# A prologue re-chained per output, w1 cut 3 x 128 + 64, and w2 in seven row halves: two parallel blocks on one Trainium2 core

## The chip, the cores and the metric

The kernel runs on one core of a Trainium2 chip (trn2). The metric is the device time of one execution in microseconds; before the change the median of three runs is 178.09 us. Engines are named as in the profile: PE is TensorE (PEld its weight loads), DVE is VectorE, ACT is ScalarE, POOL is GpSimd, SP is SyncE; SPq and ACTq are the two queues that start DMAs here.

## The reference

Token count S = 2048, width D = 448, 16 heads of 28, MLP width 1792, all in bf16. `_A_ref` is a linear attention with a softmax feature map, `_B_ref` a shifted mixing block with an MLP; both read the same normalised input.

```python
xn = _layernorm(x)
return x + _A_ref(xn, A_wqkv, A_w_phi, A_wo) + _B_ref(xn, B_w1, B_w2, B_w3, B_w4)

# A: q, k, v from xn @ wqkv, per head:
pq, pk = q @ w_phi, k @ w_phi
phi_q = concat(softmax(pq), softmax(-pq)); phi_k = concat(softmax(pk), softmax(-pk))
kv = phi_k^T @ v; z = sum_s phi_k
o = (phi_q @ kv) / (phi_q @ z + 1e-6); A = o @ wo

# B: (c = 112; g0..g3 are the four feature quarters, each shifted by its own number of tokens)
h = gelu(layernorm(xn) @ w1)
g0 = h[:, 0:c] one token later;  g1 = h[:, c:2c] one token earlier
g2 = h[:, 2c:3c] two later;      g3 = h[:, 3c:] two earlier
x1 = xn + concat(g0, g1, g2, g3) @ w2
B = x1 + gelu(layernorm(x1) @ w3) @ w4
```

The kernel normalises xn once and uses it for both, since a second normalisation of a normalised row is nearly the identity.

## The kernel before

The 2048 tokens are 16 tiles of 128; four tiles are a group of 512. Every operation goes through a `Recorder`: the Python order of the calls is each engine's order. `solve` works out the waits from what each operation reads and writes. For SBUF it keeps 32-byte pieces of a row, apart for the upper and lower 64 partitions but no finer than that; for PSUM it keeps whole banks. `mm` is line 203, `tr` (a transpose on PE) line 207, `act` 211, `ew` (DVE and POOL) 215, `dma_t` (a DMA transpose) 218, `dma` 221.

PE works in two row halves of 64: two matmuls with different halves run side by side. `lap_pair` splits the 448 rows of a contraction into chunks of 128 at rows 0, 128, 192 and 320 (the second and third overlap), so that an output costs seven half matmuls, four in one half and three in the other. A pair of outputs is played as two steps: the lower rows of the first beside the upper rows of the second, then the rest. A bank written from one row half has to be done before the other half adds to it; `solve` makes that a wait of PE on itself.

The prologue normalises x (`ln1_stats`, `ln1_apply`): per tile DVE takes the statistics (BATCH_NORM_STATS2, BATCH_NORM_AGGREGATE into `mv`), POOL adds epsilon and raises to the power -1/2 (`ln_scale`, into `rs`), and DVE applies both (TENSOR_SCALAR into `xn`). In the kernel before, the statistics of tile i+1 stand on DVE before the apply of tile i (but for tile 3):

```python
for i in range(10):
    ln1_stats(i, 1, 0)
    if i not in (0, 4):
        ln1_apply(dve, i - 1)
```

Tiles 0 to 11 are transposed on PE (`xn_T`) and copied to `xnT` by ACT; tiles 12 to 15 by four DMA transposes on SPq (`xn_Td`). Out of `xnT` come v (`v_pair`, `v_out`: 12 of 16 tiles here), w1 (`w1_pair`, `w1_out`: four chunks of 112 features by four groups of tokens, gelu on ACT, into `hT`), and the folded weights w_q·w_phi and w_k·w_phi (`fold_pair`, FO). `spin` is dummy matmuls at the start. SPq holds, in this order: loads of x and wv, eight DMA transposes of wqkv (`load_wT`), the four `xn_Td`, then `load_rest`: w2, w3, wo, w4.

Then come eight passes (`ps`), each with a pair of k tiles, a quarter of a q group, and one side job: a pair of w2 tiles (`w2_pair`, four chunks of 112 features in halves of 64 and 48 rows, the token shift being only another column of `hT`) or of the last v tiles. The rest interleaves w3 pairs, the attention numerators and the final sums, and ends with the stores.

The lines that the prediction's steps touch are `ln1_stats`, `ln1_apply` and `ln_scale` (DVE and POOL, line 215), `xn_Td` and `load_rest` (SPq, 218 and 221), `w1_out` (ACT, 211), and the first w1 matmul of group 3, which needs tiles 12 to 15.

Of the kernel before, what the change touches and what calls it, by code (L numbers as in the profile page):

```python
# [9 lines left out]
F32 = mybir.dt.float32  # L10
# [213 lines left out]
def bass_parallel_sum__linear_kernel_hedgehog__mixer_s_mlp__prompt_kernel(  # L224
# [5 lines left out]
    assert (S, D, H, DH, F) == (2048, 448, 16, 28, 1792)  # L230
    NT, NG, KC, NC, NM, FC, HP = 16, 4, 4, 4, 4, 14, 32
    CR = 112
    SHIFTS = [1, -1, 2, -2]
    HW = S + 16
    x2d, out2d = A_x[0], out[0]

    es = ExitStack()
    with es:
# [3 lines left out]
        def region(name, nbytes):  # L242
            nbytes = -(-nbytes // 64) * 64
            total[0] += nbytes
            h = es.enter_context(nc.sbuf_tensor(name, [128, nbytes // 2], BF16))
            R.track(h, nbytes)
            return h

        def view(h, cols, dt=BF16, at=0):
            a = h[:, at // 2:at // 2 + cols * DTB[dt] // 2]  # L250
            return a if dt == BF16 else a.bitcast(dt)
# [13 lines left out]
        xn = new("xn", NT * 512).rearrange("p (t d) -> p t d", t=NT)  # L265
        xnT_r = region("xnT", KC * S * 2)
        xnT = view(xnT_r, KC * S).rearrange("p (c s) -> p c s", c=KC)
        hT_r = region("hT", NM * HW * 2)
        hT = view(hT_r, NM * HW).rearrange("p (m s) -> p m s", m=NM)
        phik_r = region("phik", NT * 1024 * 2)  # L270
        phik = view(phik_r, NT * 1024).rearrange("p (t g e) -> p t g e", t=NT, e=HP)
        vaug_r = region("vaug", NT * 512 * 2)
        vaug = view(vaug_r, NT * 512).rearrange("p (t c) -> p t c", t=NT)
        gT = new("gT", 2 * KC * 512).rearrange("p (b c s) -> p b c s", b=2, c=KC)
        eq_lo = new("eq_lo", NC * 2 * 1024).rearrange("p (c s f) -> p c s f", c=NC, s=2)
# [7 lines left out]
        w1 = view(w1_r, KC * D).rearrange("p (c d) -> p c d", c=KC)  # L283
        w2 = new("w2", NM * D).rearrange("p (m d) -> p m d", m=NM)
        wo = new("wo", KC * D).rearrange("p (c d) -> p c d", c=KC)
        w3 = new("w3", KC * F).rearrange("p (c f) -> p c f", c=KC)
# [13 lines left out]
        rs = new("rs", NT * 8, F32).rearrange("p (t c) -> p t c", t=NT)  # L300
        st2 = new("st2", NT * 8, F32).rearrange("p (t c) -> p t c", t=NT)
        mv2 = new("mv2", NT * 8, F32).rearrange("p (t c) -> p t c", t=NT)
# [47 lines left out]
        def load_lap(dst, src, engs=("SP", "SP")):  # L350
            for h in range(2):
                R.dma(dst[:, 2 * h:2 * h + 2, :], src[192 * h:192 * h + 256, :].rearrange("(c p) d -> p c d", p=128), engs[h])

        load_x(0, 1)
        load_x(1, 1, "ACT")
        load_x(2, 1)
        load_lap(wv, A_wqkv[:, 896:1344], ("ACT", "SP"))
        load_x(3, 1, "ACT")
        load_x(4, 2)
        load_x(6, 2)  # L360

        def load_wT(t):
# [6 lines left out]

        def load_rest():  # L370
            R.dma(w2[0:CR, :, :], B_w2.rearrange("(m p) d -> p m d", p=CR))
            load_lap(w3, B_w3)
            load_lap(wo, A_wo)
            R.dma(w4[:, :, :], B_w4.rearrange("(c p) d -> p c d", p=128))

        vp = vaug.rearrange("p t (h e) -> p (t h) e", e=HP)

        R.op("ACT", lambda e: e.preload_act_table_set("gelu_apprx_tanh_and_others"), [], [])
        load_lap(w1, B_w1, ("ACT", "ACT"))
        load_x(8, 4, "ACT")  # L380
        load_x(12, 4, "ACT")
        R.dma(wphi[0:CR, :, :], A_w_phi.rearrange("(c q) e f -> (q e) c f", q=4), "ACT")
        R.ew(pool, "memset", ident[:, :], 0.0)
# [4 lines left out]
        R.ew(pool, "memset", hT[:, :, 0:2], 0.0)  # L388
        R.ew(pool, "memset", hT[:, :, S + 2:S + 4], 0.0)
        busy = gT[:, 0, 0, 0:256]  # L390
# [130 lines left out]

        def v_out(i, b, eng="ACT"):
            vd = vaug[:, i:i + 2, :].rearrange("p t (h e) -> p t h e", e=HP)[:, :, :, 0:DH]
            vs = two(2 * b)[:, :, 0:D].rearrange("p t (h e) -> p t h e", e=DH)
            if eng == "ACT":
                R.act(vd, vs, ACT.Copy)
            else:
                R.ew(dve, "tensor_copy", vd, vs)

        def w1_pair(g, m, b):  # L530
            return lap_pair([banks[2 * b + k][0:CR, :] for k in range(2)],
                         lambda k, kc, lo, hi: w1[lo:hi, kc, CR * (m + k):CR * (m + k) + CR],
                         lambda k, kc, lo, hi: xnT[lo:hi, kc, 512 * g:512 * g + 512])

        def w1_out(g, m, b):
            R.act(hT[0:CR, m:m + 2, 2 + 512 * g:2 + 512 * g + 512], two(2 * b)[0:CR, :, :], ACT.Gelu_apprx_tanh)

        def w2_pair(i, b):
            def side(k, lo, hi):
                r = []  # L540
                for m in range(NM):
                    c0 = 2 + 128 * (i + k) - SHIFTS[m]
                    r.append((banks[2 * b + k][:, 0:D], hT[lo:hi, m, c0:c0 + 128], w2[lo:hi, m, :]))
                return r
            return (lambda: row_pairs(side(0, 0, 64), side(1, 64, CR), True),
                    lambda: row_pairs(side(1, 0, 64), side(0, 64, CR)))

# [172 lines left out]

        for i in range(10):
            ln1_stats(i, 1, 0)
            if i not in (0, 4):
                ln1_apply(dve, i - 1)
            if i == 3:
                ln1_apply(dve, 3)
        phi_blocks()

        ln1_stats(10, 2, 0)
        ln1_apply(dve, 9)  # L730
        ln1_stats(12, 2, 0)
        ln1_apply(dve, 10)
        ln1_apply(dve, 11)
        ln1_stats(14, 1, 0)
        ln1_apply(dve, 12)
        ln1_apply(dve, 13)
        ln1_stats(15, 1, 0)
        ln1_apply(dve, 14)
        ln1_apply(dve, 15)
        for i in range(12, NT):  # L740
            xn_Td(i)
        load_rest()
        late_3()

        vps = {i: v_pair(i, b) for i, b in ((0, 2), (2, 3), (4, 3), (6, 2), (8, 2), (10, 3))}
        wps = {(g, m): w1_pair(g, m, b) for g, m, b in ((0, 0, 0), (0, 2, 1), (1, 0, 0), (1, 2, 1), (2, 0, 0),
                                                        (2, 2, 1), (3, 0, 0), (3, 2, 2))}
        fps = {(t, m): fold_pair(t, m, b) for t, m, b in ((1, 0, 2), (1, 2, 3), (0, 0, 1), (0, 2, 3))}

        def V(i, k):  # L750
            return (vps[i][k],)

        def W(g, m, k):
            return (wps[g, m][k],)

        def FO(t, m, k):
            return (fps[t, m][k],)

        spin(19, 256)
        play([(xn_T, 0, 0), (spin, 3, 256), (xn_T, 1, 1), (spin, 4, 256), V(0, 0), (xn_T, 2, 0), V(0, 1), (xn_T, 3, 1),  # L760
              (spin, 2, 256), V(2, 0), (v_out, 0, 2), W(0, 0, 0), (xn_T, 4, 2), V(2, 1), (v_out, 2, 3),
              W(0, 2, 0), (xn_T, 5, 2), W(0, 0, 1), (xn_T, 6, 3), W(0, 2, 1), (xn_T, 7, 2), (w1_out, 0, 0, 0),
              (w1_out, 0, 2, 1), V(4, 0), V(6, 0), V(4, 1), (v_out, 4, 3), V(6, 1), (v_out, 6, 2),
              W(1, 0, 0), (xn_T, 8, 3, 2), W(1, 2, 0), W(1, 0, 1), (xn_T, 10, 3, 2), W(1, 2, 1),
              (w1_out, 1, 0, 0), (w1_out, 1, 2, 1), V(8, 0), V(10, 0), V(8, 1), (v_out, 8, 2), V(10, 1),
              (v_out, 10, 3), W(2, 0, 0), W(2, 2, 0), FO(1, 0, 0), W(2, 0, 1), (w1_out, 2, 0, 0), FO(1, 0, 1),
              FO(1, 2, 0), W(2, 2, 1), (w1_out, 2, 2, 1), FO(1, 2, 1), W(3, 0, 0), FO(0, 0, 0), W(3, 2, 0),
              FO(0, 0, 1), FO(0, 2, 0), W(3, 2, 1), (w1_out, 3, 2, 2), W(3, 0, 1), (w1_out, 3, 0, 0), FO(0, 2, 1)])

# [10 lines left out]
        for ps in range(8):  # L780
            k, q = k_pair(2 * ps, 1), q_pair(ps // 2, 2 * (ps % 2), 0)
            kind, i = side[ps]
            w = {"w": w2_pair, "v": v_pair}[kind](i, 2)
            k[0]()
            if ps > 2:
                kv_tile(2 * ps - 6)
                kv_tile(2 * ps - 5)
            w[0]()
            k[1]()
            for s in range(2):  # L790
                k_exp(2 * ps, 1, s)
            q[0]()
            w[1]()
            if kind == "w":
                w2_out(i, 2)
            if kind == "v":
                v_out(i, 2, "DVE" if i == 12 else "ACT")
            q[1]()
            for s in range(2):
                q_exp(2 * ps, 0, s)  # L800
            k_norm(2 * ps)
            if kind == "w" and i < 8:
                w2_norm(i)
            for t in g_at.get(ps, ()):
                g_apply(t)
                g_T(t)
# [91 lines left out]
```

## Time and profile before

| | us |
|---|---|
| runs | 178.50, 178.09, 177.61 (median 178.09) |
| span of the profiled execution, first to last instruction | 175.9 |
| median of the runs less that span | 2.2 |
| PE busy | 170.8 (97%) |
| DVE / ACT / POOL busy | 110.0 / 82.5 / 93.7 |

The execution that was profiled has a span of 175.9 us. Its whole time is that span and the start and end that lie around it, which the profile doesn't show; the median run is 2.2 us over the span, and that is taken for what lies around. The busy time of PE counts dummy matmuls too. Times in the trace are microseconds from the start of the span. In the rows, a shape 64\*128 is 64 rows by 128 columns of weights; xN is a number of instructions, and what stands in square brackets is the idle time of the engine before the first of them and who ended it.

### The profile page before, as it was taken

The page shows a single profiled execution, that of the slowest core. Times are in us where ns is not written, and L with a number is a line of the kernel's source. Part 1 is how long each engine was busy: PE and PEld are TensorE (multiplying, and loading weights), DVE is VectorE, ACT ScalarE, POOL GpSimd, SP SyncE. Part 2 cuts the span into 40 slices and gives each one's busy share as a digit, 9 for nine tenths or more (in the row PEclk, how much of TensorE's full clock was granted, in tenths as well). Part 3 has the DMA queues.
Part 4 walks back from the last instruction along what each step waited for, and adds up shares of the span by engine and source line. Part 5 has one row for each costly group of instructions (what it writes and reads, how often), then busy time and mean ns, then how long its engine had stood idle before and what let it go on. Part 6 is the DMA issues. An engine that isn't in the chain of part 4 may idle for free.

```text
span 175.9 us, 5042 instructions
## 1 busy us (share of the span) xinstructions
PE 170.8 (97%) x2198; PEld 94.7 (54%) x2198; DVE 110.0 (63%) x252; ACT 82.5 (47%) x92; POOL 93.7 (53%) x130
## 2 busy tenths in 40 slices
PE   7899999998999999999999999999999999999993
PEld 4466557744565555665554554554545545545551
DVE  4799906699899697615776981644427415474621
ACT  2368874997779877926324422223214222224000
POOL 3666670016799999860358489460620723523740
PEclk9999999999999999999999999999999999999999
DMA  5994158990001120121011372134611310311331
GB/s 172 330 240 79 35 97 255 390 345 15 0 4 30 34 60 4 30 55 39 4 34 40 79 74 59 48 82 89 93 30 57 82 34 0 86 30 30 86 100 34
DMA packets 32981, 14.87 MB, mean 85 GB/s; under 512 B 24704, under 2 KB 32448, under 8 KB 32960
## 3 DMA queue, kind: packets, MB, share of 16 engines
q1 hardware_dynamic: 30192, 12.64, 29.6%
q10 hardware_dynamic: 2768, 1.92, 3.4%
q8 instruction: 17, 0.28, 0.7%
q14 instruction: 4, 0.03, 0.1%
HBM read 7.08 MB, written 1.84 MB: 51 GB/s over the span
## 4 chain that ended last, share of the span: by engine, by line
PE 91%; DVE 6%; issue 1%; POOL 0%; ACT 0%; DVEq 0%
PE bank L203 90%; DVE vaug L215 1%; DVE st L215 1%; DVE ksum L215 1%; PE bank L207 1%; DVE xn L215 1%; DVE mv L215 0%; ACT xnT L211 0%; POOL rs L215 0%; DVE rks L215 0%; DVEq L176 0%; DVE gT L215 0%; POOL mv L215 0%
## 5 line engine op out<-in xcount | busy, mean ns | idle before, releaser
L211 ACT ACTIVATE phik<-bank 128x1024 bf16<-128x1024 f32 (+1 forms) x44 | 42.3, 984 | 62.4 <-PE bank L203 62.4
L203 PE MATMUL bank<-gT,w 64*128 64x512 bf16 x392 | 50.1, 377 | 0.0
L215 DVE TENSOR_TENSOR vaug<-bank,vaug 128x464 f32<-128x464 f32 (+3 forms) x65 | 32.6, 512 | 23.0 <-PE bank L203 21.4
L203 PE MATMUL bank<-w,phik 64*128 64x448 bf16 (+1 forms) x420 | 45.0, 349 | 0.0
L215 POOL TENSOR_TENSOR xnT<-vaug 128x196 bf16<-128x196 f32 (+1 forms) x32 | 18.1, 585 | 46.8 <-DVE vaug L215 46.8
L203 PEld LDWEIGHTS bank<-w,phik 64*128 64x128 bf16 (+1 forms) x420 | 21.7, 94 | 21.2 <-issue 0.4
L215 POOL TENSOR_TENSOR phik<-phik,rks 128x1792 bf16<-128x1792 bf16 x8 | 25.7, 3212 | 10.8 <-DVE rks L215 10.8
L203 PEld LDWEIGHTS bank<-gT,w 64*128 64x128 bf16 x392 | 18.6, 94 | 17.0 <-ACT hi L211 0.3
L215 POOL TENSOR_TENSOR vaug<-xn,xtok 128x448 f32<-128x448 bf16 x16 | 16.2, 1031 | 0.2 <-DVE vaug L215 0.2
L215 DVE TENSOR_REDUCE ksum<-phik 128x64 f32<-128x1792 bf16 x8 | 16.0, 2006 | 0.0
L203 PE MATMUL bank<-w,hT 64*128 64x448 bf16 (+1 forms) x128 | 15.0, 349 | 0.5 <-DVE vaug L215 0.5
L215 DVE RECIPROCAL vaug<-bank 128x16 f32<-128x16 f32 x16 | 4.1, 257 | 18.0 <-PE bank L203 18.0
L203 PE MATMUL bank<-xnT,wpq 64*128 64x512 bf16 x112 | 14.9, 376 | 0.0
L203 PE MATMUL bank<-xnT,w 64*112 64x512 bf16 x112 | 14.8, 380 | 0.0
L203 PE MATMUL bank<-wpk,xnT 64*128 64x448 bf16 x112 | 13.4, 349 | 0.0
L203 PE MATMUL bank<-wo,xnT 64*128 64x448 bf16 (+1 forms) x106 | 13.4, 349 | 0.0
L215 DVE TENSOR_TENSOR xn<-bank,xn 128x512 bf16<-128x512 f32 (+1 forms) x16 | 9.2, 616 | 6.3 <-PE bank L203 6.3
L203 PE MATMUL bank<-wv,xnT 64*128 64x448 bf16 x112 | 13.0, 350 | 0.1
L215 POOL TENSOR_TENSOR rs<-mv,mhalf 128x1 f32<-128x1 f32 (+2 forms) x18 | 12.2, 679 | 1.5
L215 POOL TENSOR_SCALAR g_tok<-xn,rs 128x512 bf16<-128x512 bf16 x16 | 12.1, 767 | 0.2
L211 ACT ACTIVATE xnT<-bank 128x512 bf16<-128x512 bf16 x12 | 7.0, 603 | 6.3 <-PE bank L207 6.3
L215 DVE BATCH_NORM_STATS2 st<-xtok 128x6 f32<-128x448 bf16 x16 | 9.8, 615 | 0.0
(62 smaller groups left out, 168.0 us busy)
## 6 DMA issues: line engine op xcount, KB each, us to landing
w<-in_B_w_dram SPq DMA_DIRECT2D x2, 896.0 KB, 7.1
out_dram<-vaug SPq DMA_DIRECT2D x15, 112.0 KB, 1.9
w<-in_B_w_dram SPq DMA_DIRECT2D x1, 1568.0 KB, 12.0
xtok<-in_A_x_dram ACTq DMA_DIRECT2D x2, 448.0 KB, 7.3
xtok<-in_A_x_dram SPq DMA_DIRECT2D x2, 224.0 KB, 5.7
w<-in_B_w_dram ACTq DMA_DIRECT2D x2, 224.0 KB, 5.8
wo<-in_A_wo_dram SPq DMA_DIRECT2D x2, 224.0 KB, 8.4
w<-in_B_w_dram SPq DMA_DIRECT2D x1, 392.0 KB, 3.8
```

The lines of the kernel that those rows point to most:

```text
L203: self.op("PE", lambda e: e.matmul(out, lhsT, rhs, start=start, stop=stop, skip_group_check=True), [out], [lhsT, rhs], tile=self._tile(lhsT))
L207: self.op("PE", lambda e: e.transpose(out, in_, ident), [out], [in_, ident], tile=self._tile(in_))
L211: self.op("ACT", lambda e: e.activation(out, in_, func, **kw), [out], [in_] + aps)
L215: self.op(eng, lambda e: getattr(e, name)(out, *args, **kw), [out], aps)
```

## The change

It changes four things.

1. w1 is computed for features 0 to 383 in three chunks of 128 (`z_h` for tiles 0 to 3 one tile at a time, `z_w1` for groups 1 to 3), and for features 384 to 447 with tokens as rows (`z_rest`): 64 columns for each tile, read at tokens two further on, gelu into `hR`, and one DMA transpose for eight tiles (`rest_T`) into `hRT`.
2. A chunk of 128 features now crosses the borders of the shift quarters at 112, 224 and 336. So rows 64 to 127 of each chunk are copied within SBUF, shifted, by six DMAs on SPq for each half of the tokens (`h_shift`). w2 takes seven row halves for each tile in place of eight.
3. The prologue is played as one chain (`zip_in`): the lower rows of each output beside the upper rows of the output before. The normalisation's instructions are put into that chain (`L`), and five of the v copies go to DVE.
4. Loads change places: w1 and x(3) to other slots, `load_w2` behind `rest_T(0)`, w3 and w4 later, wo late into the buffer of wv.

```diff
-        load_lap(wv, A_wqkv[:, 896:1344], ("ACT", "SP"))
-        load_x(3, 1, "ACT")
-        load_x(4, 2)
+        load_half(wv, wv_d, 0, "ACT")
+        load_half(wv, wv_d, 1)
+        load_half(w1, B_w1, 0, "ACT")
+        load_x(3, 1)
+        R.op("ACT", lambda e: e.preload_act_table_set("gelu_apprx_tanh_and_others"), [], [])
+        load_half(w1, B_w1, 1)
+        load_x(4, 2, "ACT")
         load_x(6, 2)
+        load_x(8, 4, "ACT")
+        load_x(12, 4)
+        R.dma(wphi[0:CR, :, :], ...)
...
+        def zip_in(make):
+            prev, n4 = tail[0] if tail[0] else (None, True)
+            lo = make(LO, KCS[0] if n4 else (0, 1, 3)) if make else []
+            hi = prev(HI, KCS[0] if n4 else KCS[1]) if prev else []
+            for k in range(max(len(lo), len(hi))):
+                for step in (lo[k:k + 1], hi[k:k + 1]):
+                    for mms in step:
+                        for out, l, r, first in mms:
+                            R.mm(out, l, r, first, False)
+            tail[0] = (make, not n4) if make else None
...
+        def z_rest(h, b):
+            def make(rows, kcs):
+                lo, hi = rows
+                return [[(banks[b][:, 64 * j:64 * j + 64],
+                          xnT[lo:hi, kc, 1024 * h + 128 * j + 2:1024 * h + 128 * j + 130], w1[lo:hi, kc, REST:D],
+                          rows == LO and n == 0 and j == 0) for j in range(8)] for n, kc in enumerate(kcs)]
+            return make
...
+        def rest_T(h):
+            R.dma_t(hRT[:, 4 * h:4 * h + 4, :], hR[:, 512 * h:512 * h + 512])
+
+        def h_shift(gg):
+            for m, r0, r1, q in ((0, 64, 112, 0), (0, 112, 128, 1), (1, 64, 96, 1), (1, 96, 128, 2), (2, 64, 80, 2),
+                                 (2, 80, 128, 3)):
+                s0 = max(0, 1024 * gg + SHIFTS[q])
+                s1 = min(S, 1024 * gg + 1024 + SHIFTS[q])
+                c0 = OFF + s0 - SHIFTS[q]
+                R.dma(hT[r0:r1, m, s0:s1], hT[r0:r1, m, c0:c0 + s1 - s0])
 
         def w2_pair(i, b):
-            def side(k, lo, hi):
+            def side(k, hi, rest):
                 r = []
-                for m in range(NM):
-                    c0 = 2 + 128 * (i + k) - SHIFTS[m]
-                    r.append((banks[2 * b + k][:, 0:D], hT[lo:hi, m, c0:c0 + 128], w2[lo:hi, m, :]))
+                for m in range(NH):
+                    if hi:
+                        h = hT[64:128, m, 128 * (i + k):128 * (i + k) + 128]
+                    else:
+                        c0 = OFF + 128 * (i + k) - SHIFTS[m]
+                        h = hT[0:64, m, c0:c0 + 128]
+                    lo = 64 * hi
+                    r.append((banks[2 * b + k][:, 0:D], h, w2[lo:lo + 64, m, :]))
+                if rest:
+                    r.append((banks[2 * b + k][:, 0:D], hRT[lo:lo + 64, i // 2, :], w2[lo:lo + 64, NH, :]))
                 return r
...
-        for i in range(10):
-            ln1_stats(i, 1, 0)
-            if i not in (0, 4):
-                ln1_apply(dve, i - 1)
...
-        for i in range(12, NT):
-            xn_Td(i)
-        load_rest()
...
         spin(19, 256)
...
+        play([L(("s", 0), ("s", 1), ("a", 0), ("s", 2), ("a", 1), ("s", 3), ("a", 2), ("a", 3)),
+              (xn_T, 0, 0), (spin, 3, 256), (xn_T, 1, 1), ZV(0), ZV(1), (xn_T, 2, 0), ZH(0), EV(0),
+              L(("s", 4), ("a", 4)), (xn_T, 3, 0), ZV(2), EV(1, "DVE"), ZH(1),
+              L(("s", 5), ("a", 5)), (xn_T, 4, 0), ZV(3), ZH(2), EV(2),
+              L(("s", 6), ("a", 6)), (xn_T, 5, 0), ZV(4), EV(3), ZH(3), EV(4, "DVE"),
+              L(("s", 7), ("a", 7)), (xn_T, 6, 0), ZV(5), (w1_out, 0, 0, 2), (w1_out, 0, 2, 4, 1),
+              L(("s", 8), ("s", 9), ("a", 8), ("a", 9)), ZV(6), EV(5), (xn_T, 7, 0), ZV(7), EV(6, "DVE"), (phi_blocks,),
+              L(("s", 10, 2), ("a", 10), ("a", 11)), (xn_T, 8, 0, 2),
+              ZW(1, 0), EV(7), ZW(1, 1), ZW(1, 2), Z(z_rest(0, 7)), (w1_out, 1, 0, 2),
+              L(("s", 12, 2), ("a", 12), ("a", 13)), (xn_T, 10, 0, 2), ZV(8), (w1_out, 1, 2, 4, 1), (rest_out, 0, 7), (h_shift, 0),
+              ZV(9), EV(8, "DVE"),
+              L(("s", 14, 2), ("a", 14), ("a", 15)), *[(xn_Td, i) for i in range(12, NT)], (rest_T, 0), (load_w2,),
+              (late_3,), ZV(10), EV(9), ZV(11), EV(10, "DVE"), ZW(2, 0), EV(11), ZW(2, 1), FO(1, 0, 0), FO(1, 0, 1), ZW(2, 2), (w1_out, 2, 0, 2),
+              FO(1, 2, 0), FO(1, 2, 1), ZW(3, 0), (w1_out, 2, 2, 4, 1), (load_lap, w3, B_w3), FO(0, 0, 0), ZW(3, 1), FO(0, 0, 1),
+              ZW(3, 2), (w1_out, 3, 0, 2), FO(0, 2, 0), Z(z_rest(1, 5)), (w1_out, 3, 2, 4, 1), (h_shift, 1), FO(0, 2, 1), Z(None), (rest_out, 1, 5),
+              (rest_T, 1), (load_w4,)])
...
+            if ps == 5:
+                load_lap(wo, A_wo)
```

`ZV(i)` is v of tile i, `ZH(t)` the three chunks of w1 of tile t, `ZW(g, m)` a chunk of w1 of group g, `EV` the copy of a v tile out of PSUM. `load_half` and `load_lap` issue the same DMAs by halves.

## The prediction

> **What bounds the kernel now.** I read the page first, then the trace in order of time: the prologue on VectorE and GpSimd, the queue of SP, the waits of TensorE, and stretches of the last microseconds for the clock.
>
> ```profile
> PE 170.8 (97%) x2198; PEld 94.7 (54%) x2198; DVE 110.0 (63%) x252; ACT 82.5 (47%) x92; POOL 93.7 (53%) x130
> PE 91%; DVE 6%; issue 1%; POOL 0%; ACT 0%; DVEq 0%
> ```
>
> TensorE is busy for 97% of the span and carries 91% of the chain that ended last, so columns taken from it count, provided that its operands still come in time. Who delivers them in the prologue is in the timeline of VectorE (first fence) and GpSimd (second):
>
> ```profile
> 8.67 0.62 DVE L215 BATCH_NORM_STATS2 st<-xtok 128x6 f32<-128x448 bf16 x1
> 9.32 0.18 DVE L215 BATCH_NORM_AGGREGATE mv<-st 128x2 f32<-128x6 f32 x1
> 9.42 0.60 DVE L215 BATCH_NORM_STATS2 st<-xtok 128x6 f32<-128x448 bf16 x1
> 10.05 0.18 DVE L215 BATCH_NORM_AGGREGATE mv<-st 128x2 f32<-128x6 f32 x1
> 10.45 0.41 DVE L215 TENSOR_SCALAR xn<-xtok,mv,rs 128x512 bf16<-128x512 bf16 x1 [0.22 <-POOL rs L215]
> ...
> 22.64 0.41 DVE L215 TENSOR_SCALAR xn<-xtok,mv,rs 128x512 bf16<-128x512 bf16 x1 [0.72 <-POOL rs L215]
> ```
>
> ```profile
> 9.59 0.19 POOL L215 TENSOR_SCALAR mv<-mv 128x1 f32<-128x1 f32 x1 [1.29 <-DVE mv L215]
> 9.87 0.55 POOL L215 TENSOR_TENSOR rs<-mv,mhalf 128x1 f32<-128x1 f32 x1
> ```
>
> Tile 4 begins at 8.67 and is applied by 10.86: 2.19 us, of which 0.95 (9.50 to 10.45) is the trip to GpSimd. In that gap VectorE does the statistics of tile 5. So tiles follow each other every 1.1 us, and tile 15 is done at 23.05. The timeline of SP shows what comes behind it:
>
> ```profile
> 6.29 10.96 SPq L218 DMA_TRANSPOSE hi<-in_A_wqkv_dram  x8
> 20.57 5.48 SPq L218 DMA_TRANSPOSE xnT<-xn  x4
> 26.09 1.63 SPq L221 DMA_DIRECT2D w<-in_B_w_dram  x3
> ```
>
> The four transposes of tiles 12 to 15 take 1.3 us each on the queue; the last is issued at 24.8 and lands at 27.3, by the DMA rows 2.7 us from issue to landing:
>
> ```profile
> out_dram<-vaug SPq DMA_DIRECT2D x15, 112.0 KB, 1.9
> w<-in_B_w_dram SPq DMA_DIRECT2D x1, 392.0 KB, 3.8
> xnT<-xn SPq DMA_TRANSPOSE x4, 2.7
> ```
>
> TensorE starts w1 of group 3, which needs them, at 27.70 with next to no wait:
>
> ```profile
> 27.70 1.07 PE L203 MATMUL bank<-xnT,w 64*112 64x512 bf16 x8
> ```
>
> So the cover of this chain is only some 0.4 us thick.
>
> **The change, part by part.**
>
> *TensorE's columns.* 28 matmuls of 448 columns take 2.85 us (15.01); without the last one's 0.35 that is 0.093 each, and by columns 0.106 for 512. w1 loses 28 of 112 half matmuls of 512 columns: 2.97. The token rows add 112 of 64 columns. Sixteen transposes of 64 columns take 0.40, the last one 0.19, so 0.014 each: 1.57. w1 gains 1.4 us. w2 goes from 128 to 112 halves: 16 x 0.093 = 1.5 us. The per-tile form of w1 has the same columns and four times the weight loads, which lie beside matmuls. Extra waits of TensorE on itself, about 27 hand-overs in the chain, are 0.03 to 0.2 us each (0.2 is one step of a row half, two times 0.093): V(0)'s second half began 0.06 after the first one's last matmul had ended (8.12 + 0.35 to 8.53). All of this lies ahead of w1 of group 3. What ends there is decided below, and TensorE waits anyway, so gain and loss there are both worth nothing; with that cover gone, it would be 1.4 less about 1.
>
> *VectorE's order.* The built order of the changed kernel has, from tile 4 on, statistics and apply of the same tile next to each other, with a wait on GpSimd between; nothing else stands in the gap. Five copies of v (from the 128x896 cast of 1.06 and the 128x224 of 0.38: 0.61 each) join the same queue. x(3) moves from third on ACT's queue (landed at 6.14) to fourth on SP's; by the landings beside it at 6.9, so tile 3 is done at 9.1 instead of 8.75. Then, in order: tile 4, 2.2, 11.3; copy, 11.9; tiles 5 and 6, 16.3; copy, 16.9; tile 7, 19.1. Tiles 8 and 9 overlap by one step: two statistics (1.6), the second trip (about 1.0), one apply (0.4): 3.05, 22.15. Copy and mask product (0.38), 23.15. Tiles 10 and 11 have their statistics together and one trip for both: 15.52 to 18.22 for the same work in the trace, then 0.7 for two applies, so 3.45: 26.6. Tiles 12 and 13: 30.05. Copy: 30.65. Tiles 14 and 15: 34.1. That is 11 us later than 23.05.
>
> *SP's queue.* Six shifted copies now stand before the four transposes. The first waits for the gelu of group 1. That needs: tile 9 at 22.15, transposes 0.4, then three chunks of w1 less the last half, 2.4, gelu 1.03, some 0.2 for semaphores: 26.2. Each second copy waits for the landing of the one before, since both touch the same rows' half. A copy inside SBUF is not in the trace: the nearest row is the 112 KB store with 1.9 us; ends are 1.5 (the 56 KB store) and 2.6 (112 KB load). I take 1.9, for its 96 KB or less with no queue before it: landings at 28.1, 30.5, 32.9, the last issue done at 33.4. Then transposes at 33.4, 34.7, 36.0 and 37.3; tile 15 (34.1) is not in their way any more. The last lands 2.7 later: 40.0. **Group 3's w1 starts at 40.0 in place of 27.7: +12.3** (with 1.5: 38.7; with 2.6: 42.1; without any copies: tile 15 at 34.1, two transposes, 37.8).
>
> *Loads.* `rest_T(0)` is issued at 38.6, w2 at 39.9. By the 3.8 us row it lands at 43.7, and the first w2 matmul is due at 45: just hidden. w3 and w4 (7 and 12 us) are needed 20 us later and more; wo, into the place of wv, not before the final sums. The second six copies (from about 44 to 52) serve w2 tiles from 7 on.
>
> *From there on.* Behind group 3's start lay 3.7 us until the first k matmul (31.41). Now there are half the second token rows, single-sided ends and waits on itself: about 4.3, +0.6. In the passes w2 saves 1.5, but at 41.03 TensorE already waited 0.48 for VectorE, which feeds the banks there; so I take 1.2.
>
> *The clock.* TensorE will stand idle from about 36 to 40. Of such a stand the trace has only its end: the last matmul starts at 173.16, and
>
> ```profile
> core 0: us, PE busy (x) PEld busy (x) DVE busy (x) ACT busy (x) POOL busy (x), PEclk, DMA share, GB/s
> 1.20:4.90 3.70, 3.65 (x18) 2.53 (x19) 2.26 (x6) 1.28 (x1) 1.80 (x9) 1.00 0.85 249
> 175.00:176.00 1.00, 0.00 (x0) 0.00 (x0) 0.00 (x0) 0.00 (x0) 0.00 (x0) 0.84 0.04 10
> ```
>
> a mean clock of 0.84 in the last stretch is half speed for its last 0.3 us, so the clock fell some 2.5 us after the last matmul. At the start 18 dummy matmuls took 3.70 us, 0.21 each, against 0.11 for those at 5.9. A fall would thus cost up to half of 3.7, 1.9 us; none costs 0. Four microseconds are longer than 2.5, but that one row says nothing of a stand with work on both sides. I take half, 0.9. The Trainium skill ("TensorE: Matmul & The Clock Gate", Part 1) says that the clock halves after an idle window of about 3.4 us that runs freely, and warns of gaps as long between bursts. By that rule a stand of 4 us holds a whole window about once in six, an estimate from that page, and the sum would mostly be 189.8. By the row alone the fall would be sure, and the sum 191.7.
>
> Sum: 175.9 + 12.3 + 0.6 - 1.2 + 0.9 = 188.5 of span. The span of before stands 2.2 under the median of the runs; I keep that: **190.7 us**.
>
> **The rivals.**
>
> *The normalisation ends last, not the copies on SP.* If copies land in 1 us or less, the transposes of 14 and 15 wait for tile 15 and land at 37.8: 2.2 less, 188.5, or 187.6 with no fall of the clock. For it: the copies are small. Against: every DMA in the trace needs 1.5 or more. Chance 0.13.
>
> *w2 lands late.* w3's 1.8 MB go out right behind w2 and share its engines. If w2 needs 7.1 as the w3 loads did, the first w2 matmul waits until 47: +2, 192.7. It decides from 5.1 us on. Against: w2 was first in the same row of loads before, and landed in 3.8. Chance 0.08.
>
> *Faster: the trip to GpSimd stays hidden.* If the prologue were bound by TensorE alone, w1 and w2 would give 2.9 and the single chain would lose about 1: 176.2. It decides at about 1.4 us per tile from tile 4 on, so that tile 15 were applied by 24. Only a shorter trip could do that, and nothing in the change shortens it: 2.2 for a tile alone is also what tile 0 shows (3.22 to 5.45). Chance 0.03. That the change doesn't do what it says would be this case's opposite: token rows at 0.03 in place of 0.014 each, which eats w1's gain and, under the wait, costs nothing.
>
> **How the numbers follow.** The forecast has 0.76, the rivals 0.13, 0.08 and 0.03. The range goes from 187.0 (normalisation last, no fall of the clock, half a microsecond of error) to 193.5 (copies at 2.6, or w2 late). A measurement of this kernel can tell about 0.5% from no change. All cases but one are slower by 4% or more: faster 0.03, same 0.01, slower 0.96.
>
> **What would show it.** Right: applies of single tiles 2.2 us apart or more, each with some 0.9 idle released by POOL `rs`; tile 15 at about 34; three gaps on SPq released by DMAs of `hT`; the first w1 matmul of group 3 at about 40 after an idle TensorE of some 4 us; TensorE's busy time in the passes 1.5 shorter. Wrong: tile 15 applied before 30, a w1 start before 37, or a second idle stretch before the first w2 matmul.

## The result, and the profile after

The changed kernel takes 194.13 us (median of four runs, 191.76 to 194.4) beside 178.18 for the kernel before: a ratio of 1.086 (95% interval 1.080 to 1.093), 16 us more. The forecast was 190.7, in a range up to 193.5: the direction and the place were right, the size was 3.4 us short. The profiled execution took 194.26 us and has a span of 192.5. Three of the four runs took 194.0 to 194.4 at a mean granted clock of 0.973, the fourth 191.76 at 0.982, which is about one stretch of 3.41 us less at half speed.

From the page of the changed kernel: busy times, the granted clock of TensorE in 40 slices of 4.8 us, and the chain that ended last.

```profile
PE 175.0 (91%) x2323; PEld 92.9 (48%) x2323; DVE 113.3 (59%) x257; ACT 80.8 (42%) x95; POOL 92.3 (48%) x131
...
PEclk9999979966999999999999999999999999999999
...
PE 78%; DVE 8%; DMA 4%; POOL 3%; SPq 2%; ACT 2%; issue 1%; DVEq 0%
```

TensorE's share of the chain falls from 91% to 78%; DMAs, SP's queue, VectorE and GpSimd now stand in it. The clock was lowered in two places, about 23 to 27 us and 40 to 47 us. The busy time of TensorE rises by 4.2 us although it has fewer columns to do: a matmul at half speed counts as busy for twice as long (in the run with all three edits below, whose clock never fell, the same matmuls are busy for 170.0).

The timeline of VectorE, start and length in us:

```profile
7.91 0.63 DVE L215 BATCH_NORM_STATS2 st<-xtok 128x6 f32<-128x448 bf16 x1 [1.34 <-DMA xtok<-in_A_x_dram]
...
9.77 0.41 DVE L215 TENSOR_SCALAR xn<-xtok,mv,rs 128x512 bf16<-128x512 bf16 x1 [0.72 <-POOL rs L215]
...
11.89 0.41 DVE L215 TENSOR_SCALAR xn<-xtok,mv,rs 128x512 bf16<-128x512 bf16 x1 [0.95 <-POOL rs L215]
...
14.53 0.41 DVE L215 TENSOR_SCALAR xn<-xtok,mv,rs 128x512 bf16<-128x512 bf16 x1 [0.95 <-POOL rs L215]
...
16.65 0.41 DVE L215 TENSOR_SCALAR xn<-xtok,mv,rs 128x512 bf16<-128x512 bf16 x1 [0.95 <-POOL rs L215]
...
33.33 0.74 DVE L215 TENSOR_SCALAR xn<-xtok,mv,rs 128x512 bf16<-128x512 bf16 x2 [1.10 <-POOL rs L215]
```

The first row is the late x(3). In the next ones the trip to GpSimd, hidden behind the next tile's statistics before, stands open as 0.95 us of idle in each tile; a tile alone takes 2.1 us and one with a copy behind it 2.6. Tile 15 is done at 34.06, where the forecast had 34.1.

The timeline of SP, then what TensorE waited for longest (total, times, longest), then its first matmul of group 3's w1:

```profile
28.34 8.07 SPq L221 DMA_DIRECT2D hT<-hT  x6
36.46 5.24 SPq L218 DMA_TRANSPOSE xnT<-xn  x4
41.74 1.26 SPq L218 DMA_TRANSPOSE hRT<-gT  x1
43.05 2.95 SPq L221 DMA_DIRECT2D w<-in_B_w_dram  x5
```

```profile
PE bank L203 <- DMA xnT<-xn: 7.6, 1, 7.6
```

```profile
43.15 1.46 PE L203 MATMUL bank<-xnT,w 64*128 64x512 bf16 x6 [7.56 <-DMA xnT<-xn]
```

All four transposes stand behind six shifted copies, though the first two of their tiles had been normalised since 30.2. Group 3's w1 starts at 43.15, 15.45 us later than before; the first k matmul follows at 49.45, 18.04 later.

Stretches of the changed kernel, cut where the clock record changes, each 3.41 us long. The columns wanted are PE busy with its matmuls, and PEclk (third from the right):

```profile
core 0: us, PE busy (x) PEld busy (x) DVE busy (x) ACT busy (x) POOL busy (x), PEclk, DMA share, GB/s
...
16.41:19.83 3.42, 2.36 (x42) 1.18 (x39) 2.20 (x6) 2.38 (x4) 0.94 (x3) 1.00 0.51 95
19.83:23.24 3.41, 1.71 (x34) 0.83 (x36) 2.62 (x8) 0.89 (x3) 1.49 (x4) 1.00 0.02 5
23.24:26.65 3.41, 3.41 (x19) 1.51 (x15) 2.23 (x8) 1.51 (x3) 0.90 (x2) 0.50 0.00 0
33.49:36.90 3.41, 1.98 (x42) 1.22 (x36) 3.20 (x5) 1.05 (x2) 2.33 (x3) 1.00 0.13 31
36.90:40.31 3.41, 0.00 (x0) 0.00 (x0) 0.00 (x0) 0.00 (x0) 0.00 (x0) 1.00 0.54 108
40.31:43.73 3.42, 0.58 (x4) 0.33 (x6) 0.00 (x0) 0.00 (x0) 0.00 (x0) 0.50 0.57 115
43.73:47.14 3.41, 3.41 (x34) 1.74 (x30) 0.24 (x1) 0.60 (x1) 0.00 (x0) 0.50 0.73 159
```

A window that was half busy (1.71 of 3.41) is followed by one at half speed, a window busy for 1.98 is not, and an empty one is. The first fall hits w1 of group 1, on which the shifted copies wait; the second hits w1 of group 3.

### The profile page after: what moved, and what is told of

It reads as the page before. It is cut to its first block, busy times and chain, and to the rows that moved or that the text cites. A ratio compares the mean times of both kernels' runs of the same rounds, so it can differ in the third digit from the quotient of the medians.

```text
span 192.5 us, 5319 instructions
## 1 busy us (share of the span) xinstructions
PE 175.0 (91%) x2323; PEld 92.9 (48%) x2323; DVE 113.3 (59%) x257; ACT 80.8 (42%) x95; POOL 92.3 (48%) x131
## 4 chain that ended last, share of the span: by engine, by line
PE 78%; DVE 8%; DMA 4%; POOL 3%; SPq 2%; ACT 2%; issue 1%; DVEq 0%
PE bank L203 78%; DMA xtok<-in_A_x_dram 3%; DVE st L215 2%; POOL rs L215 2%; DVE xn L215 2%; SPq L218 2%; DMA xnT<-xn 1%; DVE vaug L215 1%; DVE ksum L215 1%; DVE mv L215 1%; ACT hT L211 1%; POOL mv L215 1%; SPq L221 1%; DVE wpk L215 1%; ACT xnT L211 1%
## 5 line engine op out<-in xcount | busy, mean ns | idle before, releaser
L215 DVE TENSOR_TENSOR vaug<-bank,vaug 128x464 f32<-128x464 f32 (+3 forms) x65 | 32.6, 512 | 23.0 <-PE bank L203 21.3
L203 PE MATMUL bank<-wv,xnT 64*128 64x448 bf16 (+1 forms) x218 | 32.4, 353 | 1.4 <-ACT xnT L211 0.7
L203 PE MATMUL bank<-xnT,w 64*128 64x128 bf16 (+1 forms) x147 | 19.6, 334 | 7.8 <-DMA xnT<-xn 7.6
L203 PEld LDWEIGHTS bank<-gT,w 64*128 64x128 bf16 x392 | 17.7, 94 | 17.8 <-ACT phik L211 0.4
L203 PEld LDWEIGHTS bank<-wv,xnT 64*128 64x128 bf16 (+1 forms) x218 | 12.1, 94 | 11.5 <-ACT xnT L211 1.6
L203 PEld LDWEIGHTS bank<-xnT,w 64*128 64x128 bf16 x147 | 9.5, 102 | 12.0 <-issue 8.9
L215 POOL TENSOR_SCALAR mv<-mv 128x1 f32<-128x1 f32 (+2 forms) x17 | 3.5, 203 | 20.1 <-DVE mv L215 19.8
L211 ACT ACTIVATE hT<-bank 128x1024 bf16<-128x1024 f32 (+1 forms) x8 | 6.4, 811 | 15.0 <-PE bank L203 14.8
L203 PE MATMUL bank<-w,hT 64*128 64x448 bf16 x96 | 12.1, 349 | 0.5 <-DVE vaug L215 0.5
L215 POOL TENSOR_TENSOR rs<-mv,mhalf 128x1 f32<-128x1 f32 (+2 forms) x17 | 11.7, 689 | 1.4
```

What stands on the lines that cost most here:

```text
L203: self.op("PE", lambda e: e.matmul(out, lhsT, rhs, start=start, stop=stop, skip_group_check=True), [out], [lhsT, rhs], tile=self._tile(lhsT))
L211: self.op("ACT", lambda e: e.activation(out, in_, func, **kw), [out], [in_] + aps)
L215: self.op(eng, lambda e: getattr(e, name)(out, *args, **kw), [out], aps)
```

## The experiments

Two theories of where the 16 us come from. The forecast's: VectorE's order and the copies on SP's queue, one behind the other, delay group 3, and a lowered clock adds to it. The rival: the single chain itself (single-sided ends, waits of TensorE on itself) costs a good part. The table has the marks of each profiled execution in us: end of tile 15's apply, first shifted copy, first of the four transposes, first w1 of group 3, first k matmul; then the time of the run or median.

| kernel | tile 15 | copies | transposes | group 3 | first k | time |
|---|---|---|---|---|---|---|
| before | 23.05 | none | 20.57 | 27.70 | 31.41 | 178.18 |
| changed | 34.06 | 28.34 | 36.46 | 43.15 | 49.45 | 194.13 |
| statistics ahead | 29.06 | 26.26 | 34.73 | 41.48 | 47.70 | 192.5 |
| copies behind | 33.91 | 39.45 | 29.77 | 38.53 | 45.74 | 194.63 |
| finer pieces | 33.14 | 25.88 | 30.42 | 38.02 | 44.99 | 189.79 |
| half-row dummies | 32.93 | 25.68 | 33.78 | 41.92 | 49.05 | 194.1 |
| full-row dummies | 33.22 | 25.95 | 34.02 | 40.82 | 45.20 | 190.0 |
| all three | 26.54 | 31.46 | 24.51 | 31.59 | 35.97 | 181.42 |
| all three, order kept | 34.39 | 37.95 | 29.41 | 38.06 | 44.09 | 188.94 |
| reordered | 24.47 | 28.73 | 21.12 | 28.68 | 33.20 | 179.2 |
| eight dummies | 33.61 | 26.34 | 34.42 | 41.13 | 47.46 | 192.85 |
| x(3) back | 33.02 | 27.30 | 35.93 | 42.57 | 48.47 | 193.62 |

The reordered kernel, the eight dummies and x(3) back are medians of several runs; the others of the experiments are single runs. Two things vary from one execution to the next without any edit that bears on them: when x(3) has come (with the changed kernel's loads, tile 3 is applied by 9.10 in one trace and 10.29 in another), and whether the clock falls near 23 (it did in the changed kernel's trace, not in that of the copies behind). The changed kernel's own times lie 2.6 us apart, so a smaller difference of a single run is no evidence by itself; what counts there are the marks in its trace.

**Statistics one tile ahead of the applies.**

```diff
-              L(("s", 4), ("a", 4)), (xn_T, 3, 0), ...
-              L(("s", 5), ("a", 5)), (xn_T, 4, 0), ...
+              L(("s", 5), ("a", 4)), (xn_T, 3, 0), ...
+              L(("s", 6), ("a", 5)), (xn_T, 4, 0), ...
```

> The changed kernel (194.3 us with a span of 192.5 in its profile), with one edit: the statistics of the next tile or pair stand ahead of the apply again, from tile 4 on; the copies on SP and all of TensorE's work stay. Theory (the trip to GpSimd in VectorE's order and, behind it, the copies on SP set the prologue): tile 15 is applied by about 27 instead of 34; tile 9 about 3 us earlier, so the first shifted copy starts near 24.5 instead of 28.3, the chain of six copies still takes 8 us, and w1 of group 3 starts at about 38.5 to 39.5 instead of 43.2. TensorE then stands idle longer (from about 31), the clock falls there as before: 189.5 to 191.5 us. If VectorE's order alone set the end, group 3 would start at 31 and the time be 183. Rival (the new chain of matmuls itself costs the time): no more than 1 us less, 193 to 194.

Measured: 192.5, one above the expected range. VectorE gives back 5.0 us (tile 15 at 29.06), and 1.75 of them arrive at the first k matmul. The copies still stand in front; the first went out at 26.26 and not at 24.5, since the clock fell again:

```profile
17.98:21.40 3.42, 1.66 (x36) 0.96 (x30) 3.32 (x11) 1.52 (x4) 2.21 (x5) 1.00 0.29 54
21.40:24.81 3.41, 3.41 (x19) 1.59 (x15) 3.31 (x10) 1.27 (x3) 1.10 (x3) 0.50 0.00 0
```

With 1.66 us of work in the window before it, group 1's w1 ran at half speed here too. With the copies in front, the order alone is worth little.

**The first six copies behind the transposes, `rest_T` and w2.**

```diff
-              ... (w1_out, 1, 2, 4, 1), (rest_out, 0, 7), (h_shift, 0),
+              ... (w1_out, 1, 2, 4, 1), (rest_out, 0, 7),
...
-              ... *[(xn_Td, i) for i in range(12, NT)], (rest_T, 0), (load_w2,),
+              ... *[(xn_Td, i) for i in range(12, NT)], (rest_T, 0), (load_w2,), (h_shift, 0),
```

> The changed kernel with one edit: the first six shifted copies stand behind the four transposes, the transpose of the token rows and the w2 load on SP's queue. Theory: the transposes wait for tile 15 alone (34.1), group 3 starts at about 37.5 instead of 43.2, but the copies now run from about 39 to 48 and the first w2 matmul needs the last of them: it starts at about 49 as before (50.2). The wait only moves: 192 to 196 us. If the copies were short of mattering anywhere, the time would be 5.5 less, 188.5. Rival (the matmul chain itself): 194, with no wait moved.

Measured: 194.63. The waits of TensorE:

```profile
PE bank L203 <- DMA xnT<-xn: 3.4, 1, 3.4
PE bank L203 <- DMA hT<-hT: 2.5, 1, 2.5
```

The wait is split, not removed: the four transposes now hold for the late tiles, and w2 for copies that started only at 39.45. The clock fell in two places as well (37.6 to 44.4, 51.3 to 54.7), but not near 23, though nothing ahead of that place was changed.

**Pieces of 16 partitions in `solve`**, so that copies which touch different partitions don't wait for each other.

```diff
-        halves = [h for h in (0, 1) if p0 < 64 * h + 64 and p1 > 64 * h]
+        halves = range(p0 // 16, (p1 - 1) // 16 + 1)
```

> The changed kernel with one edit in the recorder: SBUF is kept in pieces of 16 partitions instead of 64, so that the second copy of each pair no longer waits for the first one's landing. Theory: six issues back to back, 28.3 to 31.8, transposes at 31.8, 33.1, 34.4 and 35.7, group 3 starts at about 38.4 instead of 43.2: 4.7 less, and 2.0 less again if the clock does not fall in the shorter stand: 187.5 to 189.8 us. If the copies' time were hidden behind the normalisation: 194. Rival (the matmul chain itself): 194.

Measured: 189.79. SP's timeline:

```profile
25.88 4.50 SPq L221 DMA_DIRECT2D hT<-hT  x6
30.42 5.22 SPq L218 DMA_TRANSPOSE xnT<-xn  x4
```

Six copies take 4.5 us of the queue in place of 8.07. That is 3.6 of the 6.0 us by which the transposes start earlier. The other 2.5 come from ahead of the copies and not from the edit: this execution had x(3) 0.9 earlier, and no fall of the clock near 23. In the stand the clock fell here too (36.6 to 43.4). Beside the changed kernel's run of 191.76, the gain is 2.0 and not 4.3.

**Dummy matmuls of 64 rows**, 8 ahead of the transposes of tiles 8 and 9, 38 ahead of group 3's w1.

```diff
-              L(("s", 10, 2), ("a", 10), ("a", 11)), (xn_T, 8, 0, 2),
+              L(("s", 10, 2), ("a", 10), ("a", 11)), (spin64, 8), (xn_T, 8, 0, 2),
...
-              FO(1, 2, 0), FO(1, 2, 1), ZW(3, 0), ...
+              FO(1, 2, 0), FO(1, 2, 1), (spin64, 38), ZW(3, 0), ...
```

> The changed kernel with dummy matmuls of 256 columns on one row half put into two stands of TensorE: 8 ahead of the transposes of tiles 8 and 9, 38 ahead of w1 of group 3. Nothing else is changed. Theory (the clock fell at 23.2 because the window before it was half idle, and at 40.3 because of the long stand): with both filled the granted clock stays at 1, the three chunks of w1 of group 1 take 2.4 instead of 4.2, all behind them starts 1.8 earlier, and the work behind the second stand runs 2.0 faster: 190.0 to 190.8 us. If a half-idle window does not matter, only the second part is won: 192.3. If the clock's fall costs nothing: 194.

Measured: 194.1, not the 190.0 to 190.8 expected. The clock was kept at 23 and the copies went out at 25.68, but the second stand had it at half speed, in spite of matmuls without a gap:

```profile
33.24:36.65 3.41, 2.03 (x31) 1.35 (x28) 2.22 (x3) 1.02 (x1) 2.02 (x2) 1.00 0.38 88
36.65:40.06 3.41, 3.41 (x19) 2.37 (x17) 0.00 (x0) 0.00 (x0) 0.00 (x0) 0.50 0.49 100
40.06:43.48 3.42, 3.42 (x22) 2.38 (x21) 0.00 (x0) 0.00 (x0) 0.00 (x0) 0.50 0.64 153
```

The first window is 59% busy, 1.1 of its 2.03 us with half-row dummies (from 35.52 on), and the clock fell; and two windows full of them did not bring it back. The dummies, twice as long at half speed, then ran on to about 42 and delayed group 3 themselves.

**The same with all 128 rows**, 8 and 45 of them.

> As the run before with dummy matmuls (8 ahead of the transposes of tiles 8 and 9, 45 ahead of w1 of group 3), but on all 128 rows instead of one half. There the clock held at the first stand but fell at 36.7 and stayed at half until 46.9, though TensorE's rows were 100% busy. Theory (the clock follows the rows in use, so half-row matmuls count as half): now it holds in both stands, the first shifted copy starts near 25.7, w1 of group 3 at about 40.5 to 41, and all behind it runs at full speed: the first k matmul 5.5 later at about 46.3 (49.5 in the changed kernel), 190 to 191.5 us. Rival (long waits on a semaphore pull the clock down whatever is queued): 193.5 to 194.5 again.

Measured: 190.0, with the clock kept:

```profile
34.16:37.58 3.42, 2.10 (x25) 1.79 (x26) 1.58 (x2) 0.72 (x1) 1.39 (x2) 1.00 0.50 110
37.58:40.99 3.41, 3.41 (x33) 2.84 (x32) 0.00 (x0) 0.00 (x0) 0.00 (x0) 1.00 0.49 98
```

From group 3's w1 to the first k matmul it is 4.38 us at full speed (40.82 to 45.20), 6.30 in the changed kernel. That is the price of the second fall: 1.92.

**Statistics ahead, finer pieces, and the first copies behind the transposes, with w2's load moved ahead of all of them.**

```diff
+        load_w2()
...
-              L(("s", 14, 2), ("a", 14), ("a", 15)), *[(xn_Td, i) for i in range(12, NT)], (rest_T, 0), (load_w2,),
+              L(("a", 14), ("a", 15)), *[(xn_Td, i) for i in range(12, NT)], (rest_T, 0), (h_shift, 0),
```

> The changed kernel with the next tile's statistics ahead again (as in the first experiment), SBUF kept in pieces of 16 partitions (as in the third), the first six copies behind the four transposes and the token rows' transpose, and w2 loaded right behind the eight transposes of wqkv. TensorE's work and its order are the changed kernel's. Theory: no wait on SP is left in front of group 3; transposes at about 26, 27.3, 28.6, 29.9, landing by 32.5; the rest is VectorE (five v copies in its queue, x(3) late) and ACT's order; the first k matmul at about 37 to 38 (31.4 before, 49.5 in the changed kernel): 182 to 184 us, so 10 to 12 of the 16 us come back. Rival (the chain of matmuls itself costs most of it): 188 or more, with w1 of group 3 started by 33 all the same.

Measured: 181.42, the clock at full speed throughout. SP's timeline:

```profile
24.51 5.60 SPq L218 DMA_TRANSPOSE xnT<-xn  x4
30.15 1.27 SPq L218 DMA_TRANSPOSE hRT<-gT  x1
31.46 3.75 SPq L221 DMA_DIRECT2D hT<-hT  x6
```

12.7 of the 16 us come back, where the order alone gave 1.6, the finer pieces 4.3 (part of it the earlier start above) and the moved copies nothing.

**The same with VectorE's order kept as changed**, so that only the order stands ahead of the transposes.

> Fine keys for the copies, transposes ahead of the copies and w2's load early, as in the run with all three edits (181.42 us), but with VectorE's order as the changed kernel has it: so the order alone stands in front of the transposes, and nothing of SP. If the trip to GpSimd is exposed as the forecast says (2.2 us for a tile alone), tile 15 is applied at 33.5 to 34.5, the first of the two late transposes goes out then, group 3's w1 starts at 37.5 to 38.5 (forecast: 37.8 without any copies) and the kernel takes 186 to 189 us: 5 to 8 us more than with the statistics ahead. Rival (the order costs little once SP's queue is free; TensorE's own chain sets the pace): 181 to 184 us.

Measured: 188.94, 7.5 more than with the statistics ahead. VectorE's applies of the last two tiles, and TensorE's first w1 of group 3:

```profile
33.66 0.73 DVE L215 TENSOR_SCALAR xn<-xtok,mv,rs 128x512 bf16<-128x512 bf16 x2 [1.10 <-POOL rs L215]
```

```profile
38.06 1.20 PE L203 MATMUL bank<-xnT,w 64*128 64x512 bf16 x6 [1.87 <-DMA xnT<-xn]
```

The start at 38.06 is the forecast's "without any copies" (37.8). So the open trip to GpSimd costs 6.5 us at this place (38.06 against 31.59; 0.75 of it is VectorE waiting ahead of a v copy for TensorE, whose clock was at half speed from 21.3 to 28.1) and the clock, at half speed from 38.4 to 41.8, another 1.65 (6.03 from there to the first k matmul, against 4.38); behind that 0.6 come back.

**The chain in another order**: all three edits, x(3) third on ACT's queue, and single steps of the chain moved.

```diff
-        play([L(("s", 0), ("s", 1), ("a", 0), ("s", 2), ("a", 1), ("s", 3), ("a", 2), ("a", 3)),
...
+        play([L(("s", 0)), L(("s", 1)), L(("a", 0)), L(("a", 1)), (spin, 3, 256), L(("s", 2)), L(("s", 3)), L(("a", 2)),
+              (xn_T, 0, 0), L(("a", 3)), L(("s", 4)), (xn_T, 1, 1), ZV(0), (xn_T, 2, 0), ZH(0), L(("s", 5)), ...
+              ... *[(xn_Td, i) for i in range(12, NT)], ZW(2, 0), ZW(2, 1), (rest_out, 0, 7), EV(9, "DVE"), ...
```

> All three edits, with the chain's items written in another order as well (statistics one tile ahead from the start, the v copies later and more of them on ACT, w1 of group 2 ahead of the last v tiles) and x(3) third on ACT's queue as before the change. If the prologue's loss is only one of order, the whole 16 us come back and the saved columns of w2 stay: 176.5 to 179 us, the clock kept throughout, first k matmul at 31.5 to 33.5. Rival (the single chain and its waits of TensorE on itself cost by themselves): 180 us or more, with the first k matmul behind 35.

Measured: 179.2 (ten runs), a ratio of 1.0053 to the kernel before (interval 1.0035 to 1.007). The time lies between the two expectations, the first k matmul in the range of the first. So nearly all of the 16 us are order and the waits on SP's queue, and what is left of the change does not pay for itself. From the page:

```profile
PE 169.1 (96%) x2323; PEld 92.8 (53%) x2323; DVE 112.3 (64%) x256; ACT 80.8 (46%) x96; POOL 92.8 (53%) x131
```

TensorE is 1.7 us less busy than before, but the first k matmul is 1.79 later (33.20). From there on it takes 143.5 us to the end of the span, 144.5 before: by this, w2's halves give 1.0. Up to there, matmuls other than dummies ran for 24.3 us before, 25.0 in this kernel and 25.9 with all three edits alone; dummies by themselves for 5.2, 4.1 and 4.1; and no matmul at all for 1.9, 4.1 and 5.9. So w1's 1.4 us of columns do not show in the prologue: the matmuls take 0.7 to 1.6 more in place of 1.4 less. I put that down to steps in which only one row half runs, but no run tries it by itself. In this the rival theory has a point, of 2 to 3 us and not of 16.

**Eight full-row dummies ahead of the transposes of tiles 8 and 9, and nothing else.**

```diff
-              L(("s", 10, 2), ("a", 10), ("a", 11)), (xn_T, 8, 0, 2),
+              L(("s", 10, 2), ("a", 10), ("a", 11)), (spin_all, 8), (xn_T, 8, 0, 2),
```

> The changed kernel with eight dummy matmuls of all 128 rows and 256 columns (0.9 us) ahead of the transposes of tiles 8 and 9, nothing else. In the profile of the changed kernel the window of 3.41 us before the first fall of the clock is 50% busy; with them it would be 70% or more. If a half-busy window is what lets the clock fall, w1 of group 1 runs at full speed, the first shifted copy goes out 2 us earlier (26.0 to 26.8 in place of 28.34), and the time is 191.5 to 192.6 us; the second fall, of the long stand, stays. Rival (the fall has another cause, or the 2 us are taken up further on): 193.5 to 195.

Measured: 192.85 (four runs, 192.26 to 193.21), 1.3 less than the changed kernel. In the profiled one, 192.26 us:

```profile
17.86:21.28 3.42, 2.00 (x25) 0.86 (x22) 2.18 (x7) 2.30 (x4) 1.67 (x5) 1.00 0.20 38
21.28:24.69 3.41, 3.32 (x44) 1.62 (x44) 2.76 (x8) 1.52 (x3) 0.55 (x1) 1.00 0.00 0
```

58% busy, not the 70% expected, since the windows lie elsewhere; but the fall at 23 is gone, the first copy goes out at 26.34, 2.0 earlier (0.4 of it by x(3)), and the time is 2.0 less. Of the first window the dummies fill only the last 0.3 us (they start at 20.98); without them it would be about half busy. But that the dummies are worth 2 us is not shown: two executions without any had no fall there either (copies behind, finer pieces), and the changed kernel's own run of 191.76 is faster than all four. The other three runs have a lower mean clock (0.973 against 0.982, about one window more at half speed); where it fell in them no trace shows. The median lies just above the expected range.

**x(3) third on ACT's queue again.**

```diff
-        load_half(w1, B_w1, 0, "ACT")
-        load_x(3, 1)
+        load_x(3, 1, "ACT")
+        load_half(w1, B_w1, 0, "ACT")
```

> The changed kernel with x(3) third on ACT's queue again, ahead of w1's first half. If VectorE's 1.34 us of idle for that load pass through one for one, tile 3 is applied at 8.7 to 9.1 in place of 9.77, everything behind it comes 0.7 to 1.0 us earlier, and the time is 193.0 to 193.5 us (the forecast had this step at 0.35 us late, not 1.0). Rival (w1 then lands later and takes its place, or the clock's windows swallow it): 193.9 or more.

Measured: 193.62 (four runs, 192.0 to 194.29). Tile 3 was done at 8.82 in place of 10.18, tile 15 at 33.02, 1.0 earlier, and the first copy went out 1.0 earlier (27.30). But the copies took half a microsecond longer, the transposes start 0.5 earlier, and the median is 0.5 less; between these two medians that is not told apart from nothing. Tile 3 came nearly as early in some executions without this edit (9.10 with the half-row dummies). The place of this load is not what the time hangs on.

## Why the prediction was wrong

*Right.* The mechanism: the trip to GpSimd stands open in each tile, copies on SP stand ahead of the transposes, and TensorE waits for tiles 12 to 15. The marks that were named came: applies 2.1 us apart and more, 0.95 idle each, tile 15 at 34, an idle TensorE, and no second stand ahead of w2, which landed at 47.6, before its first matmul at 50.2. w2's part, 1.2 of gain, measured 1.44 by the time from the first k matmul to the end (0.8 and 1.0 in the two kernels with a short prologue). The 4.3 us from group 3 to the first k matmul measured 4.38 at full speed. The rival that the normalisation ends last is out: the transposes waited for copies.

*Luck.* Tile 15 at 34 came by two errors that cancel. x(3) made tile 3 1.1 us late (10.18, not 9.1), and from there the forecast's steps, 25.0 us to tile 15, took 23.9; with tile 3 at 9.10, as forecast, tile 15 was done at 32.93 (half-row dummies).

*Wrong: the sum, by 4.0 us of span (192.5 against 188.5).* Three terms carry it.

1. The first shifted copy, "26.2", went out at 28.34: 2.1. The failed step is "three chunks of w1 less the last half, 2.4". I priced w1 of group 1 at the full clock; it ran from 22.9 to 27.2, mostly at half speed, since TensorE had been busy half of the window before, waiting for VectorE tile by tile. The forecast looked for a fall of the clock only in the long stand. Of the 2.1, tile 9 itself was 0.6 late (22.73, not 22.15), behind the late x(3); the other 1.5 are this step.
2. The copies: 8.1 us from the first issue to the first transpose in place of 7.2, 0.9 more. The landings that were waited for took 2.4, 2.0 and 2.0; "I take 1.9" was the lower end of what came.
3. The clock in the long stand: "I take half, 0.9" should have been the whole 1.9, 1.0 more. The stand was 7.56 us, not 4, so that it held at least one whole window of 3.41 us without work.

That the clock makes item 1 is seen in the other runs. The forecast's step from tile 9 to the first copy was 4.05 us (22.15 to 26.2). In the four traces in which the copies stand in this place and the clock did not fall there, it took 4.05 or 4.06, with dummies (half-row, full-row, eight) and without (finer pieces); in the three in which it fell, 5.6 (the changed kernel, statistics ahead, x(3) back). The same 15 matmuls in the changed kernel, then in the one with finer pieces:

```profile
23.86 3.39 PE L203 MATMUL bank<-xnT,w 64*128 64x512 bf16 x15
```

```profile
22.65 2.14 PE L203 MATMUL bank<-xnT,w 64*128 64x512 bf16 x15
```

The three terms and the rest are 2.1 + 0.9 + 0.1 (transposes) + 1.1 (43.15 to 49.45 against 4.3 + 0.9) - 0.25 (w2) = 4.0. The span stands 1.6 us under the median here, not 2.2, so 3.4 of it reached the time. In each run on record that has both, the time is 1.7 to 1.8 us over its own span; the 2.2 set the median of three runs beside the span of a single execution.

On the clock the Trainium skill ("TensorE: Matmul & The Clock Gate", Part 1) ties the lower clock, in its table of the two states, to an idle window of about 3.4 us; here a window with 1.71 us of work in it, in matmuls with no gap longer than 0.7 us, was followed by half speed, and the measurement decides. Of the two sums in the forecast the one that took the fall for sure was nearer.

The range missed too: it ended at copies of 2.6 us or a late w2, each by itself, and had no case in which the same delay makes TensorE both late and slow.

## What to carry to other kernels

When an engine that was always busy starts to wait in small pieces, price its work behind them at the lowered clock as well: add up its busy time in stretches of 3.4 us, not only the longest gap. Where the stretches lie changes from one execution to the next, so compare a step between traces with and without the fall. When several delays stand one behind the other on a path, taking one away shows little: here, by single runs, 1.6, 4.3 and nothing singly, 12.7 together; so judge a cause with the others out of the way. Columns saved need not be time saved, perhaps where the other row half has nothing to run beside: sum the time in which any matmul runs, not the matmuls.

## What the runs showed of the hardware

The granted clock followed the share of a 3.41 us window in which TensorE was busy. I cut the traces of all these kernels at the steps of their clock records, 3.41 us apart (the run with all three edits has no step and is left out). Of the windows at full speed, those that were busy for 0, 26, 27, 34, 37, 41, 43, 48, 49, 50 and 51% are followed by half speed, those for 55, 56, 57, 58, 61% and all above by full speed. The one exception is the 59% shown above, which are in part half-row dummies. That half-row matmuls count for less is what this and the two full windows of them suggest; it was not tried by itself. After a fall the clock did not come back behind a window of 83% (the kernel with the order kept, 21.3 to 24.7), and did behind one of 92% (x(3) back, 42.3 to 45.7).

A copy of 96 KB or less within SBUF, of which the trace of before had none, landed after 1.9 to 2.8 us in the first six of the changed kernel: the DMA view of the changed kernel, with KB each and median us to landing, has

```profile
hT<-hT SPq DMA_DIRECT2D x2, 96.0 KB, 2.5
...
hT<-hT SPq DMA_DIRECT2D x2, 32.0 KB, 2.0
```

so a third of the bytes saves half a microsecond, and a chain in which each copy waits for the landing before it pays the trip each time: three such waits stand in the 8.1 us of the first six. One of the second six, issued while w3 was being loaded, took 5.2.
